# Second expert layer and output of a soft mixture of experts: halves of the columns become quarters, and all first-layer work comes ahead of it

## The chip, the cores and the metric

One core of one Trainium2 chip runs one program. The metric is the device time of one execution in microseconds (us). The kernel before took 386.4 us (median of three runs, 386.28 to 388.14). A difference of 0.5% is 1.9 us.

## The reference

Block-causal attention (blocks of 64), and a soft mixture of experts on its output; the change touches only the experts and what follows them. All values are float32.

```python
# attention: B=8, H=8, S=576, D=64 -> x of (N=4608, 512), N = B*S
logits = x @ phi                                   # (4608, 32): 8 experts x 4 slots
d = softmax(logits, axis=0);  slot_input = (d.T @ x).reshape(8, 4, 512)
for e in range(8):
    h = np.maximum(slot_input[e] @ w1[e], 0.0)     # w1[e]: (512, 1024), 2 MB
    slot_out[e] = h @ w2[e]                        # w2[e]: (1024, 512), 2 MB
c = softmax(logits, axis=1)
out = c @ slot_out.reshape(32, 512)                # (4608, 512), 9.4 MB
```

## The kernel before

The kernel has two parts. The attention part runs a software pipeline over 32 pairs of heads; every operation has a due time in a table (`TM`), and a sort of these times gives each engine's order. It also makes the logits, the 32 slot inputs (`acc`, `acc4`), and `c_all`, the weights of the last softmax. The change leaves all of that alone. The second part begins at line 683; there each engine's order is the order of the Python text.

**Weights.** Both layers' weights are 32 pieces of 1 MB (128 x 2048 floats), loaded by `load_piece` on SP's queue, in the order of their numbers. Pieces 0 to 14 go to space kept free for them during the attention part. Pieces 15 to 21 go to the attention part's own buffers as these fall free. Pieces 22 to 31 go to the places of pieces that `up` has read: `use(i)` issues the next load as soon as piece i is consumed, and once all 32 are issued it puts the place into the list `free`. The first place of `free` becomes the second `hT`; the other five are the ring `stage`, from which results are written out.

**First layer.** `up(qd, nh, c)` handles four experts (`qd`), half of the 1024 hidden columns (`nh`) and a quarter of the contraction (`c`): four matmuls of 512 columns side by side, each in 32 columns of the array. After the fourth `c`, ACT applies the relu (`hr`, line 800). `turn(qd, nh)` transposes the result on PE (line 805), and DVE copies it into `hT` (line 810).

**Second layer.** `down(qd, f, u)` multiplies one of eight slices of the hidden columns, for four experts, into half `u` of the 512 output columns: four matmuls of 256 columns side by side. Sixteen such steps make one half, summed in a PSUM bank `so[u]`. `copy_so` copies it to SBUF on DVE, and `finish` folds the four groups with one matmul (line 753) and an ACT copy (`s4`, line 756).

**Output.** `emit(u, i)` multiplies `cT` (the transposed softmax weights of two batches) or `cT4` (the 64 last rows of all batches) by `s4[u]`: four banks of PSUM (`ps_x`), each in a row group of 32 of the array. ACT copies banks 0 and 2 to a buffer of `stage`, DVE banks 1 and 3, and one DMA on SP's queue writes 1 MB (i under 4) or 0.5 MB (i = 4). All four banks of `ps_x` are in use in one `emit`, so the next one waits for these copies.

**Order.** `up` of the first four experts; then their eight `down` steps for half 0; `combine` of the second four batches' softmax; `up` of the other four experts; the other eight `down` steps for half 0; and then `STEPS` spreads the sixteen `down` steps of half 1 between the five `emit` of half 0. The five `emit` of half 1 follow. `turn_c(1)`, which makes the second `cT`, stands in the second group of `down` steps for half 0.

An fp32 matmul shows as two records in the trace: a step of four matmuls is eight records.

## Time and profile before

| | |
|---|---|
| median of 3 runs | 386.4 us |
| the profiled execution's own time | 387.56 us |
| its span, first to last instruction | 385.8 us |
| share of TensorE's full clock granted, mean | 0.978 |
| PE, DVE, ACT, POOL busy | 365.4, 286.7, 278.1, 182.0 us |
| moved by DMA | 72.27 MB, of which 9.44 MB written |

The shares are means over the attention part and the experts. The experts' part is the last 60 us, from about 327 us on, and the rows below are nearly all from there. Times in the rows are us from the span's start.

### The profile page before, as it was taken

How to read it: one execution, taken by the hardware profiler on the slowest of the kernel's cores; microseconds unless marked ns; L12 is line 12 of the kernel's file. 1: busy time of each engine (PE TensorE's matmuls, PEld its weight loads, DVE VectorE, ACT ScalarE, POOL GpSimd, SP SyncE). 2: the span in 40 equal slices, each digit the busy share in tenths (PEclk: the TensorE clock that was granted, in tenths of full speed). 3: DMA queues.
4: the chain of work that ended last, by engine and by line, in shares of the span. 5: the costliest groups of instructions: out<-in, count | busy, mean ns of one | idle time of the engine just before them, and what ended most of it. 6: DMA issues, size and time to landing. Idle time of an engine off the chain costs nothing.

```text
span 385.8 us, 14041 instructions
## 1 busy us (share of the span) xinstructions
PE 365.4 (95%) x5487; PEld 241.8 (63%) x5487; DVE 286.7 (74%) x851; ACT 278.1 (72%) x883; POOL 182.0 (47%) x349
## 2 busy tenths in 40 slices
PE   7799999999999999999999999999999989999974
PEld 2466677667767776777667766766776655344542
DVE  3577779887988898889888988898889866041552
ACT  2687888988898889788888888888888854211441
POOL 5465665555555555555555555555555442010000
PEclk9699999999999999999999999999999999999995
DMA  5326366353564563535636635453332289799797
GB/s 158 93 63 209 108 216 197 101 203 98 199 206 105 201 197 98 211 92 197 216 92 211 198 102 194 119 187 97 93 95 65 88 305 358 297 426 406 290 373 329
DMA packets 28786, 72.27 MB, mean 187 GB/s; under 512 B 6832, under 2 KB 15152, under 8 KB 23600
## 3 DMA queue, kind: packets, MB, share of 16 engines
q1 hardware_dynamic: 28720, 71.38, 53.7%
q8 instruction: 43, 0.70, 0.7%
q14 instruction: 23, 0.19, 0.1%
HBM read 61.93 MB, written 9.44 MB: 185 GB/s over the span
## 4 chain that ended last, share of the span: by engine, by line
PE 89%; ACT 4%; DVE 3%; issue 2%; POOL 0%; ACTq 0%; POOLq 0%; DVEq 0%
PE x L424 19%; PE sc L312 16%; PE pt_e L386 11%; PE sc L333 11%; PE x L434 6%; PE pt_o L386 5%; PE so L819 4%; PE hp L792 4%; PE o L770 3%; PE x L553 3%; PE x L453 2%; PE x L571 2%; ACT arena L242 1%; PE x L283 1%; ACT arena L357 1%
## 5 line engine op out<-in xcount | busy, mean ns | idle before, releaser
L369 POOL TENSOR_SCALAR arena<-arena,stat 128x512 f32<-128x512 f32 (+6 forms) x288 | 152.6, 548 | 135.3 <-DVE stat L364 129.8
L357 ACT ACTIVATE arena<-sc,stat 128x512 f32<-128x512 f32 (+6 forms) x288 | 154.6, 550 | 20.9 <-DVE stat L347 18.5
L347 DVE TENSOR_REDUCE stat<-sc 128x1 f32<-128x512 f32 (+6 forms) x256 | 131.6, 541 | 4.3 <-PE sc L333 1.9
L386 PEld LDWEIGHTS pt_e<-ident,arena 64*128 64x128 f32 x800 | 63.7, 139 | 47.5 <-issue 30.9
L242 ACT COPY arena<-pt_e 128x384 f32<-128x384 f32 (+2 forms) x127 | 63.4, 500 | 24.2 <-PE pt_o L386 23.0
L386 PE MATMUL pt_e<-ident,arena 64*128 64x64 f32 x800 | 74.8, 228 | 5.0 <-ACT arena L242 3.5
L424 PE MATMUL x<-arena 128*64 128x256 f32 (+2 forms) x640 | 76.1, 384 | 0.4 <-DVE arena L244 0.4
L386 PE MATMUL pt_o<-ident,arena 64*128 64x64 f32 x800 | 74.7, 228 | 0.0
L312 PE MATMUL sc<-arena 64*128 64x512 f32 (+1 forms) x256 | 67.1, 598 | 0.8 <-ACT arena L357 0.7
L386 PEld LDWEIGHTS pt_o<-ident,arena 64*128 64x128 f32 x800 | 62.7, 139 | 0.2
L357 ACT ACTIVATION_READ_ACCUMULATOR arena<-sc,stat 128x1 f32 x288 | 61.2, 212 | 0.0
L424 PEld LDWEIGHTS x<-arena 128*64 128x64 f32 x640 | 41.0, 137 | 30.6 <-issue 18.2
L333 PE MATMUL sc<-arena 64*64 64x288 f32 (+4 forms) x768 | 45.7, 344 | 2.9 <-ACT arena L357 2.9
L333 PEld LDWEIGHTS sc<-arena 64*64 64x64 f32 x768 | 38.4, 134 | 12.1 <-issue 6.3
L242 ACT COPY arena<-pt_o 128x512 f32<-128x512 f32 (+1 forms) x63 | 33.8, 537 | 10.0 <-PE x L424 9.4
L244 DVE COPY arena<-pt_o 128x320 f32<-128x320 f32 (+1 forms) x65 | 33.9, 521 | 4.9 <-PE pt_o L386 3.0
L244 DVE COPY xT<-x 128x64 f32<-128x64 f32 (+1 forms) x42 | 19.0, 453 | 12.2 <-PE x L424 11.9
L363 DVE TENSOR_SCALAR stat<-stat 128x2 f32<-128x2 f32 (+1 forms) x96 | 26.4, 275 | 2.1 <-ACT arena L357 2.1
L434 PE MATMUL x<-arena 128*64 128x64 f32 x640 | 25.7, 227 | 0.0
L312 PEld LDWEIGHTS sc<-arena 64*128 64x128 f32 x256 | 20.6, 192 | 6.3 <-issue 2.4
L276 POOL TENSOR_SCALAR arena<-arena 128x576 f32<-128x576 f32 x32 | 21.6, 674 | 3.0 <-DMA arena<-in_k 3.0
L434 PEld LDWEIGHTS x<-arena 128*64 128x64 f32 x640 | 21.2, 137 | 2.2
(142 smaller groups left out, 343.8 us busy)
## 6 DMA issues: line engine op xcount, KB each, us to landing
arena<-in_w SPq DMA_DIRECT2D x32, 1024.0 KB, 6.7
arena<-in_k SPq DMA_DIRECT2D x32, 288.0 KB, 3.7
arena<-in_q SPq DMA_DIRECT2D x32, 288.0 KB, 3.0
arena<-in_v SPq DMA_DIRECT2D x32, 256.0 KB, 3.1
out<-arena SPq DMA_DIRECT2D x8, 1024.0 KB, 4.7
arena<-in_v SPq DMA_DIRECT2D x32, 32.0 KB, 2.7
out<-arena SPq DMA_DIRECT2D x2, 512.0 KB, 4.6
arena<-in_phi SPq DMA_DIRECT2D x1, 64.0 KB, 3.1
```

The source lines that it names most:

```text
L242: nc.scalar.copy(out=out, in_=in_)
L244: nc.vector.tensor_copy(out=out, in_=in_)
L276: nc.gpsimd.tensor_scalar(out=area(f"ks{m % NQB}"), in0=area("kr"), scalar1=SCALE, scalar2=0.0, op0=ALU.mult, op1=ALU.add)
L312: nc.tensor.matmul(scores(t + str(j)), lhsT=q[r, lo:lo + 128], rhs=k[r, 0:NC[t]], start=True, stop=True)
L333: nc.tensor.matmul(o, lhsT=a, rhs=b, start=True, stop=True)
L347: nc.vector.tensor_reduce(out=st[:, 0, u:u + n], in_=sc, axis=AX.XY if x == "8" else AX.X, op=ALU.max, negate=True)
L357: nc.scalar.activation(out=pr, in_=sc, func=AF.Exp, bias=st[:, 0, u:u + 1], accum_out=st[:, 1, u:u + 1],)
L363: nc.vector.tensor_scalar(out=st[:, 2, c], in0=st[:, 1, c], scalar1=EPS, scalar2=None, op0=ALU.add)
L369: nc.gpsimd.tensor_scalar(out=pr, in0=pr, scalar1=st[:, 2, u:u + 1], scalar2=0.0, op0=ALU.mult, op1=ALU.add)
L386: nc.tensor.transpose(out=ptb[i][:, 64 * n:64 * n + 64], in_=prob(m, x)[r, 128 * c:128 * c + 128], identity=ident[r, r],)
L424: nc.tensor.matmul(xps[m, 0][64 * j:64 * j + 64, lo:hi], lhsT=vs(m)[:, j, c, :], rhs=rhs, start=a, stop=z, skip_group_check=True,)
L434: nc.tensor.matmul(xps[m, 1][64 * j:64 * j + 64, 0:64], lhsT=vs(m)[:, j, c, :], rhs=arena[:, lo:lo + 64], start=(c == 0), stop=(c == NQ - 1),)
```

## The change

The first layer of all eight experts comes first: pieces 0 to 15 are now w1, 16 to 31 w2. The second layer and the output go by four quarters of 128 columns (`NU`, `CW`) instead of two halves of 256. `down(u, n)` handles quarter u with steps n = 0 to 15 over both groups of experts, four matmuls of 128 columns each; the last step also copies `so` to SBUF. One `emit` now covers four batches for its quarter (the two that make 1 MB before are four by half the width), and the 64 last rows of all batches go out for two quarters at a time, after quarters 1 and 3. There are still ten transfers out, eight of 1 MB and two of 0.5 MB, and 32 loads of 1 MB. The order of the end is written out in `ENDING`: a number is so many `down` steps, "f1" is `finish(1)`, "21" is `emit(2, 1)`, "c" is `turn_c(1)`. `finish` takes its bank from the pool of `up` (`ps_h`), and `emit(3, 1)` takes two banks of that pool and two of `so`'s.

```diff
-STEPS = (2, 2, 3, 3, 3, 3, 0)
+NU = 4
+CW = 128
+ENDING = (2, "f0", 2, "00", 4, "c", 2, "01", 6, 2, "f1", 2, "10", 6, "11", 6, 2, "f2", 2, "20", 6, "21", 6, "12", "f3", "30", "31", "32")
...
-        ps_o = c2.enter_context(tc.tile_pool(name="ps_o", bufs=1, space=PSUM))
+        ps_o = c2.enter_context(tc.tile_pool(name="ps_o", bufs=2, space=PSUM))
...
-            ps = ps_x.tile([128, 512], F32, tag="x", name=f"s4_ps{u}")
+            ps = ps_h.tile([128, 512], F32, tag="h", name=f"s4_ps{u}")
...
-            n = 512 if i < 4 else 256
-            pss = [ps_x.tile([128, 512], F32, tag="x", name=f"o_{u}_{i}_{g}") for g in range(4)]
-            for x in range(n // 256):
+            if (u, i) == (NU - 1, 1):
+
+                pss = [ps_h.tile([128, 512], F32, tag="h", name=f"o_{u}_{i}_{g}") for g in range(2)]
+                pss += [ps_o.tile([128, 512], F32, tag="so", name=f"o_{u}_{i}_{g}") for g in range(2, 4)]
+            else:
+                pss = [ps_x.tile([128, 512], F32, tag="x", name=f"o_{u}_{i}_{g}") for g in range(4)]
+            todo = [(cT[i][:, x, :], s4[u]) for x in range(4)] if i < 2 else [(cT4, s4[u - 1]), (cT4, s4[u])]
+            n = CW * len(todo)
+            for x, (a, c) in enumerate(todo):
...
-        def down(qd, f, u):
-            half = slice(256 * u, 256 * u + 256)
+        def down(u, n):
+            qd, f = divmod(n, 8)
+            if n == 0:
+                so[u] = ps_o.tile([128, 512], F32, tag="so", name=f"so{u}")
+            i = 16 + 4 * u + n // 4
             for g in range(4):
-                rhs = pieces[8 + f][:, g, half] if qd == 0 else pieces[24 + 4 * u + f // 2][:, 4 * (f % 2) + g, :]
                 nc.tensor.matmul(
-                    so[u][NS * g:NS * (g + 1), :], lhsT=hTs[qd][:, f, g, :], rhs=rhs,
-                    start=(qd == 0 and f == 0), stop=(qd == 1 and f == 7), tile_position=(0, NS * g),
-                )
+                    so[u][NS * g:NS * (g + 1), 0:CW], lhsT=hTs[qd][:, f, g, :], rhs=pieces[i][:, 4 * (n % 4) + g, :],
+                    start=(n == 0), stop=(n == 15), tile_position=(0, NS * g),
+                )
+            if n == 15:
+                so_sb[u] = t2.tile([128, CW], F32, tag="so_sb", name=f"so_sb{u}", bufs=2)
+                nc.vector.tensor_copy(out=so_sb[u], in_=so[u][:, 0:CW])
...
             for c in range(4):
                 up(qd, 0, c)
+                if qd == 1 and c == 1:
+                    turn(0, 1)
...
             if qd == 0:
-                for f in range(8):
-                    down(0, f, 0)
-                    if f == 0:
-                        turn(0, 1)
                 for i in range(2):
                     combine(t2, nc.vector, 1, i)
...
-        for f in range(8):
-            down(1, f, 0)
-            if f == 1:
+        for n in range(16):
+            down(0, n)
+            if n == 3:
                 turn(1, 1)
-            if f == 4:
+        steps = [(u, n) for u in range(1, NU) for n in range(16)]
+        for x in ENDING:
+            if x == "c":
                 turn_c(1)
-        copy_so(0)
-        ahead(STEPS[0])
-        finish(0, so_sb[0])
...
+            elif isinstance(x, str) and x[0] == "f":
+                finish(int(x[1]))
+            elif isinstance(x, str):
+                emit(int(x[0]), int(x[1]))
+            else:
+                for u, n in steps[:x]:
+                    down(u, n)
+                del steps[:x]
```

The host's reordering of w1, w2 and of the result is adapted; no size in bytes changes.

## Rows read from the trace of the kernel before

**Rows 1.** Table by stretches of the end of the span. Columns: stretch in us, its length, then busy us (and number of records) of PE, PE's weight loads, DVE, ACT and POOL, the granted TensorE clock, the busy share of the DMA engines, GB/s.

```profile
329.00:331.00 2.00, 2.00 (x21) 0.68 (x25) 0.00 (x0) 0.70 (x2) 0.00 (x0) 1.00 0.04 16
331.00:356.00 25.00, 24.62 (x287) 10.30 (x283) 5.83 (x23) 4.39 (x8) 1.22 (x2) 1.00 0.99 409
356.60:360.00 3.40, 3.40 (x60) 2.17 (x56) 1.29 (x2) 1.07 (x2) 0.00 (x0) 1.00 0.09 36
360.00:371.00 11.00, 9.39 (x139) 4.92 (x131) 5.76 (x11) 4.95 (x11) 0.00 (x0) 1.00 1.00 411
371.00:373.00 2.00, 1.76 (x16) 1.22 (x16) 1.16 (x2) 0.65 (x2) 0.00 (x0) 1.00 0.58 236
373.00:384.00 11.00, 6.40 (x40) 4.34 (x40) 4.23 (x8) 3.78 (x8) 0.00 (x0) 0.62 0.99 406
384.00:385.80 1.80, 0.00 (x0) 0.00 (x0) 0.00 (x0) 0.00 (x0) 0.00 (x0) 0.50 0.01 5
```

**Rows 2.** SP's queue in order of time: start, length, issuing line, what, number of transfers. Line 191 loads weights, lines 781 and 783 write results.

```profile
330.20 7.06 SPq L191 DMA_DIRECT2D arena<-in_w  x8
342.42 1.19 SPq L191 DMA_DIRECT2D arena<-in_w  x2
359.25 2.85 SPq L781 DMA_DIRECT2D out<-arena  x2
361.75 2.86 SPq L781 DMA_DIRECT2D out<-arena  x2
368.36 0.33 SPq L783 DMA_DIRECT2D out<-arena  x1
371.64 0.33 SPq L781 DMA_DIRECT2D out<-arena  x1
...
380.59 0.33 SPq L783 DMA_DIRECT2D out<-arena  x1
```

**Rows 3.** The chain that ended last, in order of time: start, length, engine, tile and line, number of records.

```profile
329.14 5.29 PE hp L792 x48
334.43 0.59 PE hT L805 x4
335.02 1.90 PE hp L792 x16
...
352.05 0.59 PE cT_ps L715 x4
352.63 0.20 PE cT_ps L725
...
355.13 0.63 PE s_ps L753 x2
...
356.76 1.08 PE o L770 x16
357.83 1.43 PE so L819 x24
359.27 1.10 PE o L770 x16
```

**Rows 4.** The same chain, earlier: matmuls with 128, 64 and 32 columns; the first two in column groups of 32 of the array, as `down`, the third with a full array of 128 weight columns.

```profile
320.57 0.35 PE x L453 x8
320.93 0.49 PE x L463 x32
327.43 0.81 PE siT_ps L696 x8
```

**Rows 5.** Instructions of the stretch from 329 to 386 us by line and shape: number, busy us and mean ns of one, idle time before them and what ended it.

```profile
L779 DVE COPY arena<-o 128x512 f32<-128x512 f32 x16 | 10.4, 687 | 12.1 <-PE o L770 12.0
L777 ACT COPY arena<-o 128x512 f32<-128x512 f32 x16 | 8.7, 588 | 11.1 <-PE o L770 7.3 <-issue 2.9 <-ACT arena L777 0.9
L779 DVE COPY arena<-o 128x256 f32<-128x256 f32 x4 | 1.6, 422 | 1.1 <-PE o L770 1.1
L861 DVE COPY so_sb<-so 128x256 f32<-128x256 f32 x2 | 0.8, 425 | 3.4 <-PE so L819 3.4
L756 ACT COPY s<-s_ps 128x256 f32<-128x256 f32 x2 | 0.7, 372 | 2.9 <-PE s_ps L753 2.9
L728 ACT COPY cT<-cT_ps 128x64 f32<-128x64 f32 x2 | 0.4, 218 | 0.0
```

**Rows 6.** Instructions in order of time, DVE and PE: start, length, engine, line, operation, out<-in, number, idle before.

```profile
328.34 0.29 DVE L699 COPY siT<-siT_ps 128x128 f32<-128x128 f32 x1 [1.51 <-PE siT_ps L696]
356.69 1.15 PE L770 MATMUL o<-s,cT 32*128 32x256 f32 x16
359.20 1.17 PE L770 MATMUL o<-s,cT 32*128 32x256 f32 x16
366.76 0.71 PE L770 MATMUL o<-s,cT 32*128 32x256 f32 x8
369.08 1.15 PE L770 MATMUL o<-s,cT 32*128 32x256 f32 x16 [0.46 <-ACT s L756]
```

**Rows 7.** Table as in rows 1, single microseconds.

```profile
356.00:357.00 1.00, 1.00 (x20) 0.50 (x16) 0.00 (x0) 0.17 (x1) 0.00 (x0) 1.00 0.68 279
360.00:361.00 1.00, 1.00 (x24) 0.45 (x20) 0.60 (x1) 0.64 (x2) 0.00 (x0) 1.00 0.94 393
375.00:376.00 1.00, 0.71 (x7) 0.63 (x8) 0.94 (x2) 0.72 (x2) 0.00 (x0) 0.84 1.10 459
```

## The prediction

> **What bounds it now.** I read the table by stretches first [rows 1]. From 331 to 356 us the DMA engines are busy 0.99 of the time, from 356.6 to 360 only 0.09, then 1.00, 0.58 for two microseconds, 0.99 to 384, and nothing in the last 1.8. So the end is a transfer of weights, a hole, and a transfer of results. PE is busy through the hole: it works off what must come before the first result. SP's queue [rows 2] says what opens and closes the hole. Line 191 loads at 330.20 and after; these are the ten pieces that wait for `up` to free places. The first result is issued at 359.25, and data moves from about 360.1 (0.94 busy in that microsecond [rows 7]), 0.85 us after the issue. The ten loads run from about 331.2 (0.99 of the 25 us from 331 on [rows 1]) to 356.7 (0.68 busy in that microsecond [rows 7]): 25.5 us, 2.55 us a megabyte.

> With these sizes the end of the kernel before can be rebuilt. Results start at 360.1, nine megabytes take 22.95 us, the second hole costs 0.42 of 2 us, 0.84: 383.9. Data ends at 384.0, the span 1.8 later. So three things set the end: when the first result is issued, whether results are then made every 2.55 us, and the two fixed lags. Two bounds follow: the loads end at 356.7 whatever is done after 330, since `up` of the first four experts frees the places at the same times in both kernels; and the results need 22.95 us behind them. No order can end before 356.7 + 22.95 + 1.8 = 381.45, 4.35 under the span.

> The chain [rows 3] shows what PE does before the first result: `up` from 329.14, transposes, `down` for half 0 in two groups, `turn_c`, the fold (0.63), the first `emit` at 356.69 [rows 6].

> **The change, part by part: the work up to the first result.** Sizes first. Six `up` steps take 5.29 us [rows 3], 0.87 each without the start, four times 0.215 us for two passes of 256 columns; so 0.107 us for 128 columns of one pass. Three old `down` steps (24 records) take 1.43 us [rows 3]: six times 0.215, and 0.14 for going from one shape of array to another. A new `down` step has half the columns. Does it take half the time? The nearest rows are line 453, 128 columns in the same column groups (0.35 us for eight records alone, start and end included), and line 463, 64 columns: 32 records in 0.49 us, 0.12 a step of eight, as long as its columns take (0.107) within a tenth [rows 4]. I take 0.215 for a new step, so 64 new steps cost what 32 old ones did; k steps in one block cost 0.215 k + 0.14.

> In the new order PE goes on at 336.7, behind the first eight `up` (335.02 + 1.90, less 0.2 in which the last matmul drains [rows 3]). Then: eight more `up`, 7.0; three `turn` of 0.59 [rows 3], 1.8, and 0.1 for the last relu; sixteen `down` steps of quarter 0, 3.45; three changes of shape that the sums don't hold yet, 0.4. That is 349.4 at most, and 349.3 is taken. Removed from this path: half the columns of the sixteen old `down` steps, and `turn_c` (0.59 + 0.20 [rows 3]). Nothing here waits for a piece: 0 to 21 have landed by 329 (DMA 0.04 busy from there [rows 1]). `combine` now stands ahead of `turn(0, 1)`'s copies on DVE, four operations of about 0.8 us; what waits behind them is the second half of `hT` for the first experts, wanted only in the fifth `down` step, five microseconds later. So I cost it at nothing. If that cover were gone it would cost the two microseconds by which `combine` outlasts the transposes.

> Then two `down` steps (0.57), `finish` (one matmul in two passes of 128 columns, 0.215, and 0.2 around it: the old 0.63 less 0.215 [rows 3]), two `down` steps. The copies of 128x128 take 0.29 on DVE [rows 6], on ACT between 0.22 (64 wide) and 0.37 (256 wide) [rows 5]; the two blocks cover each. First `emit` at 350.9, against 356.69: 5.8 us sooner. From an `emit`'s first matmul to its DMA issue it is 2.56 us now (356.69 to 359.25, 359.20 to 361.75, 369.08 to 371.64 [rows 2, 6]), two pairs of copies of 0.69 on DVE [rows 5] among it. First result issued at 353.5, before the loads have ended. The first hole is gone.

> **The work between results.** An old `emit` holds PE 1.10 us [rows 3]: four groups of 0.215 and 0.24. A new one has eight groups of 0.107, each with weights of its own, 128 columns. Line 696 loads such weights for eight records in 0.81 us, 0.10 a record [rows 4], so that load and stream take about the same; if they overlap, as they must in the old `emit` (four groups of 0.215 + 0.10 would make 1.26 before any start, and it took 1.08 to 1.10 in all), 1.10 stays. That is taken; if they don't, it is 1.10 + 8 x 0.10 = 1.9.

> [...]

> Now `ENDING`, as start times of the emits on PE. "01" comes behind 1.10, four steps 1.0, "c" 0.79, two steps 0.57: 354.35. "10" comes behind 1.10, eight steps 1.86, fold 0.42, two steps 0.57: 358.3. "11": 1.10 + 1.43, 360.85; the four banks are free then, since old emits stand 2.51 apart with the same copies [rows 6]. "20": 364.8. "21": 367.35. "12", half an `emit`, 0.66: 369.9. "f3" 0.42; its copy on ACT waits behind those of "12" (two of 0.37), and what waits behind it is "30": 371.7. Issues: 353.5, 356.9, 360.9, 363.4, 367.4, 369.9, 371.5 (half: 366.76 to 368.36, 1.60 [rows 2, 6]), 374.3, and then, as "31" has banks of its own and DVE works without a pause, 375.6 and 376.4 (+ 1.37 and + 0.84). The other banks thus save the wait for copies; I cost that at nothing, since "30" is still being sent for 2.55 us.

> Data, at 0.85 behind an issue and 2.55 a megabyte, in order: "00" 356.7 to 359.25, "01" to 361.8, "10" to 364.35, "11" to 366.9. "20" can start only at 368.25: a hole of 1.35. It ends 370.8, "21" 373.35, "12" 374.6; "30" starts at 375.15, a hole of 0.55, and with "31" and "32" ends at 381.5. The span ends at 383.3. Holes after the first result come to 1.9 us against 0.84 before: a pair of emits takes PE 6.5 us, its transfer 5.1. Of the 4.35 that the bound allows, 2.5 are won.

> **Rivals.** First, results without a hole: if a pair of emits is made faster by a microsecond than summed (the 0.14 and 0.2 around blocks overlap more), the span ends at 381.45 to 382.4, 4.35 to 3.4 under before: 382.0 to 383.0. For it speaks that most starts were counted as in isolation; against it, that they were taken from rows.

> Second, the hand-offs give it back. Twenty blocks stand between 350.9 and "30", most of them a change of shape, and each extra 0.1 us moves the end by 2.0. At 0.07 to 0.15 more (a start of 0.21 to 0.29 instead of 0.14, or copies of 0.29 that two short steps don't cover), the median is 385.3 to 386.9. The fold of 0.63 with its 0.2 around it [rows 3] shows that such sizes occur.

> [...]

> Third, slower: the weights of an `emit` are not hidden at 128 columns. "30" then starts six and a half emits later by 0.8 us each, 5.2: the span ends at 388.5, the median at 389.1. It decides from 0.69 us an emit on (0.5% slower), and gives the whole gain back at 0.39. Against it speaks the overlap in the old `emit`.

> The clock: it fell from 1.00 to 0.84 in the microsecond from 375 and then to half, after PE had work for 9.39 of 11 and 1.76 of 2 us [rows 1, 7]. The new order keeps PE in work until 374.9 or so, and I count no loss. At half clock from 371 on, "30" would be issued 1.1 later, and so would the end be.

> **How the numbers follow.** The sum is against the profiled execution: 385.8 span, 387.56 us of its own time, 1.8 around it. The median of the three runs is 386.4, so I take the difference: 386.4 - 2.5 = 383.9. Own range of this case 383.0 to 385.3. Chances: this 0.48; no hole 0.17; hand-offs 0.25; weights not hidden 0.10. From 381.8 (under the bound by 0.2) to 386.6 about 8 in 10 are held: all of the first two, most of the third, none of the last. Faster by over 0.5% (under 384.5, about what a measurement of this kernel can tell from no change): 0.17 and four fifths of 0.48, 0.56. Slower: the last, 0.09. The rest, 0.35, is within 0.5%.

> **What would show it.** In the profile after: `up` ends near 345 and the first result is issued at 353 to 354; DMA is busy without a pause from 331 to about 366.5; emits of a pair start 2.5 us apart and the first of two pairs 6.5; a short hole stands ahead of the fifth transfer. Wrong would be: an `emit` that holds PE 1.5 us or more (third rival), a new `down` step over 0.25, DMA idle between 357 and 366 (second rival), or loads that end later than 357, on which the bound rests.

## The result and the profile after

Before, the median is 386.48 us (385.94 to 388.64, 17 runs); after, 389.28 us (388.59 to 390.67, 17 runs). The ratio is 1.0064, with a 95% interval of 1.0049 to 1.0079: slower by 0.6%, where I had forecast 0.6% faster. The profiled execution of after took 389.62 us, with a span of 387.8.

Its attention part, which the change leaves alone, happened to end 0.63 us sooner: the first `up` matmul starts at 328.45 us instead of 329.07. Where I set a forecast time beside a measured one below, the forecast is moved by that. Counted from that matmul, the rest took 56.7 us before and 59.4 after; 54.2 was forecast.

TensorE's instructions from the first `emit` on, in order of time: start, length, line, tile, number of matmul records, and in brackets the idle time ahead of the group and what ended it. Line 778 is `emit`, 831 `down`, 754 the fold.

```profile
350.25 1.16 PE L778 MATMUL o<-s,cT 32*128 32x128 f32 x28
352.51 0.49 PE L778 MATMUL o<-s,cT 32*128 32x128 f32 x4 [1.10 <-issue]
...
355.30 1.23 PE L778 MATMUL o<-s,cT 32*128 32x128 f32 x32
356.46 1.29 PE L831 MATMUL so<-arena 128*32 128x128 f32 x39
358.84 0.52 PE L831 MATMUL so<-arena 128*32 128x128 f32 x9 [1.08 <-issue]
...
363.28 0.49 PE L778 MATMUL o<-s,cT 32*128 32x128 f32 x5
364.21 1.16 PE L778 MATMUL o<-s,cT 32*128 32x128 f32 x27 [0.44 <-issue]
...
368.23 0.93 PE L778 MATMUL o<-s,cT 32*128 32x128 f32 x19
369.59 0.72 PE L778 MATMUL o<-s,cT 32*128 32x128 f32 x13 [0.43 <-issue]
...
371.68 1.17 PE L778 MATMUL o<-s,cT 32*128 32x128 f32 x32
372.79 1.52 PE L831 MATMUL so<-arena 128*32 128x128 f32 x48
374.23 0.73 PE L778 MATMUL o<-s,cT 32*128 32x128 f32 x16
...
375.89 3.28 PE L778 MATMUL o<-s,cT 32*128 32x128 f32 x80 [0.51 <-ACT s L758]
```

The first `emit` stands at 350.25; 350.9 less 0.63 is 350.27. So everything up to there was summed right. An undisturbed `emit` is 32 matmul records and 1.1 to 1.2 us long, and the next block starts 1.11 behind it (371.68 to 372.79). But four blocks are cut in two, in the middle: the first `emit` after 28 of its 32, the `down` steps behind "01" after 39, "11" after 5, "20" after 19. Ahead of the second piece stands "issue", which means that the engine waited for nothing that the profile shows: no semaphore, no other engine, no bank (the one stop of another kind, ahead of the last line, waits for ACT's copy of the fold). The weight loads stop with the matmuls, which the same view of their queue shows:

```profile
352.51 0.30 PEld L778 LDWEIGHTS o<-s,cT 32*128 32x128 f32 x3 [1.29 <-issue]
358.84 0.25 PEld L831 LDWEIGHTS so<-arena 128*32 128x32 f32 x9 [1.35 <-issue]
364.21 0.42 PEld L778 LDWEIGHTS o<-s,cT 32*128 32x128 f32 x12 [0.63 <-issue]
369.59 0.53 PEld L778 LDWEIGHTS o<-s,cT 32*128 32x128 f32 x13 [0.62 <-issue]
```

What the stops do to the transfers is seen in the table by stretches, as in [rows 1, 7] (stretch, length, busy us of PE, its weight loads, DVE, ACT and POOL, granted clock, DMA share, GB/s):

```profile
353.00:361.00 8.00, 6.92 (x175) 5.36 (x179) 2.27 (x4) 2.55 (x6) 0.00 (x0) 1.00 0.99 401
361.00:364.00 3.00, 2.77 (x85) 2.26 (x81) 1.29 (x2) 1.07 (x2) 0.00 (x0) 1.00 0.20 79
366.00:368.00 2.00, 2.00 (x62) 1.64 (x55) 0.82 (x2) 0.52 (x2) 0.00 (x0) 1.00 0.68 266
370.00:372.00 2.00, 2.00 (x65) 1.68 (x63) 1.29 (x2) 1.07 (x2) 0.00 (x0) 1.00 0.06 16
```

The old hole at 357 [rows 1] is gone, as forecast. In its place stand three, of about 2.4, 0.6 and 1.9 us (length times one less the share), ahead of the third, fourth and fifth result; of these three places the forecast had a hole only at the last, of 1.35 us.

Where the stops come from is told by two lines of the page, the instructions of each engine and the DMA queues by kind. Before:

```profile
PE 365.4 (95%) x5487; PEld 241.8 (63%) x5487; DVE 286.7 (74%) x851; ACT 278.1 (72%) x883; POOL 182.0 (47%) x349
q8 instruction: 43, 0.70, 0.7%
```

After:

```profile
PE 362.5 (93%) x5891; PEld 247.8 (64%) x5891; DVE 286.7 (74%) x853; ACT 278.1 (72%) x885; POOL 182.0 (47%) x349
q8 instruction: 46, 0.75, 0.8%
```

Queue 8 carries instructions: 43 packets for 10,974 records of PE and its weight loads before, 46 for 11,782 after, one for 255 or 256 records on the mean, 16 KB each. Counted in the records of after, the four stops are 255, 256 and 256 apart, one packet's worth each. The packet with the next block starts 2.9 to 4.0 us after PE has begun the block before it (3.31, 4.02, 3.10, 2.89), and PE goes on 2.3 to 2.5 us after the packet's start (2.39, 2.31, 2.28, 2.48): 5.4 to 6.3 us a block. The new kernel uses one up sooner: an `emit` and six `down` steps are 64 + 96 = 160 records, weight loads among them, in 2.55 us (371.68 to 374.23), so 256 in 4.1. Before, an `emit` and three `down` steps held 32 + 48 = 80 in 2.51 us [rows 6], so 256 in 8.0.

A block's packet comes while the block before it runs, and this throughout the profile: of the 46 packets of after, 45 start when TensorE has begun the block before theirs, one 0.96 us ahead of that, and none a block earlier.

### The profile page after: what moved, and what is told of

Its sections match the earlier page's. It is cut to its first block, busy times and chain, and to the rows that moved or that the text cites. A ratio compares the mean times of both kernels' runs of the same rounds, so it can differ in the third digit from the quotient of the medians.

```text
span 387.8 us, 14854 instructions
## 1 busy us (share of the span) xinstructions
PE 362.5 (93%) x5891; PEld 247.8 (64%) x5891; DVE 286.7 (74%) x853; ACT 278.1 (72%) x885; POOL 182.0 (47%) x349
## 5 line engine op out<-in xcount | busy, mean ns | idle before, releaser
L428 PEld LDWEIGHTS x<-arena 128*64 128x64 f32 x640 | 41.0, 137 | 30.6 <-issue 18.2
L337 PE MATMUL sc<-arena 64*64 64x288 f32 (+4 forms) x768 | 44.9, 340 | 3.2 <-ACT arena L361 3.2
L787 DVE COPY arena<-o 128x512 f32<-128x512 f32 (+1 forms) x20 | 11.7, 632 | 16.4 <-PE o L778 16.4
(142 smaller groups left out, 360.9 us busy)
```

What stands on the lines that cost most here:

```text
L337: nc.tensor.matmul(o, lhsT=a, rhs=b, start=True, stop=True)
L428: nc.tensor.matmul(xps[m, 0][64 * j:64 * j + 64, lo:hi], lhsT=vs(m)[:, j, c, :], rhs=rhs, start=a, stop=z, skip_group_check=True,)
```

## The experiments

**The same program, shifted.** Thirty-two small matmuls, 64 records with their weight loads, at the start.

```diff
+        def pad():
+            nc.tensor.matmul(xps["w"][:, 0:64], lhsT=idle[:, 0:128], rhs=idle[:, 128:192], start=True, stop=True)
...
+        for i in range(32):
+            at(-49 + 0.01 * i, pad)
```

> 32 small matmuls on zeros are put at the very start, where PE waits for the first loads; they are 64 more PE instructions ahead of everything else. Theory A (PE runs out of instructions: they come in blocks of 256, and in the dense part it gets through a block before the next has come): the four stops of the changed kernel move up the program by 64 instructions. They stood inside emit 00 (28 of 32 records done), in the eight down steps behind emit 01 (39 of 64 done), in emit 11 (5 done) and in emit 20 (19 done); now they stand in the two down steps ahead of emit 00, in the same eight down steps but with about 7 of 64 done, in the six down steps behind emit 10 (about 20 of 48), and in the two down steps ahead of emit 20. Together 3 to 4.5 us as before, the time within 1 us of the changed kernel's 389.3. Theory B (a wait of the program itself: a bank, a copy, a buffer that is not free): the stops stay at the same matmuls of the program, the same lengths.

It took 390.08 us (389.30 to 391.06, 5 runs), ratio to before 1.0086. TensorE, as above (836 is `down`, 783 `emit` here):

```profile
350.44 0.63 PE L836 MATMUL so<-arena,hT 128*32 128x128 f32 x12
352.32 0.41 PE L836 MATMUL so<-arena,hT 128*32 128x128 f32 x4 [1.25 <-issue]
352.67 1.17 PE L783 MATMUL o<-s,cT 32*128 32x128 f32 x32
...
357.31 0.42 PE L836 MATMUL so<-arena 128*32 128x128 f32 x7
358.51 1.39 PE L836 MATMUL so<-arena 128*32 128x128 f32 x41 [0.78 <-issue]
```

The first two stops stand at the same numbers of instruction as in after, counted from the program's start, and so at other instructions: the first `emit` is whole, and the two `down` steps ahead of it are cut. Neither `emit` nor `down` stops by itself; the place in the program does it. The size did not come out as expected: the third and fourth stop are missing (their packets started 1.29 and 1.36 us after the block before had begun, instead of 3.10 and 2.89), one of under 0.5 us stands among the last emits instead, and yet the kernel is no faster than after. In its profile "30" starts 45.4 us behind the first `up` matmul, 2.0 sooner than in after, but from there to the span's end it is 13.1 us instead of 11.95. Most data has ended by 384.5, but some of the DMA engines run on to 386.2 (0.45 busy in the microsecond from 384, 0.09 in the next). Why the last transfer straggles there I can't say.

**Fewer instructions for the same `emit`.** The operands are exchanged: the 128 columns of `s4` become the weights, the four batches of `cT` the 512 moving columns. A 1 MB `emit` is 16 records instead of 64, with the same columns streamed; the host's reordering follows.

```diff
-            todo = [(cT[i][:, x, :], s4[u]) for x in range(4)] if i < 2 else [(cT4, s4[u - 1]), (cT4, s4[u])]
-            n = CW * len(todo)
+            todo = [(s4[u], cT[i].rearrange("p b s -> p (b s)"))] if i < 2 else [(s4[u - 1], cT4), (s4[u], cT4)]
+            m = 512 if i < 2 else 128
+            n = m * len(todo)
...
```

> emit with its operands exchanged: the folded result is loaded as weights once for each row group, and the softmax weights of four batches stream as 512 columns, so the 1 MB emits have 16 PE instructions instead of 64 with the same columns streamed; the result comes out transposed and the host puts it in order. Theory A: one pair of an emit and six down steps is 112 instructions in 2.5 us instead of 160; the stops shrink from 3.9 us to under 1, emit 30 starts at about 371 to 372 instead of 375.9, the time is 384.3 to 386.3. Theory B: the banks, copies and buffers are the same, the stops stay, 389. Third: the new order is slow for another cause (transfers, copies): 388 to 389.5.

It took 386.36 us (385.22 to 388.89, 10 runs): ratio to before 1.0001 [0.9978, 1.0024], 2.9 us less than after. TensorE:

```profile
350.56 0.85 PE L832 MATMUL so<-arena,hT 128*32 128x128 f32 x20
352.03 0.63 PE L832 MATMUL so<-arena,hT 128*32 128x128 f32 x12 [0.62 <-issue]
...
358.02 1.71 PE L779 MATMUL o<-cT,s 32*128 32x512 f32 x8
359.66 1.08 PE L832 MATMUL so<-arena,hT 128*32 128x128 f32 x32
...
361.10 1.14 PE L779 MATMUL o<-cT,s 32*128 32x512 f32 x8
362.18 1.52 PE L832 MATMUL so<-arena 128*32 128x128 f32 x48
```

An undisturbed `emit` is as long as before (1.14 us; the next block 1.08 behind it). With six `down` steps it is now 112 records, weight loads among them, 256 in 5.8 us. The third and fourth stop are gone. The second has shrunk and shows no idle time: in the `emit` at 358.02 the fourth row group starts 0.57 us behind the other three, 255 records behind the first stop and 2.5 us behind the start of a packet, and the next block stands 1.64 us behind instead of 1.08. The two stops left come to 1.2 us, a little more than the 1 us expected at most. The first one stays: ahead of it stand the sixteen `down` steps of quarter 0, 256 records in some 3.5 us besides the transposes between them.

**The dense blocks spread.** The `down` steps of the first four experts for quarters 0 and 1 stand between the `up` steps of the others, where a block of 256 records lasts longest (an `up` step's 16, weight loads among them, take 0.87 us [rows 3], so 256 take 13.9). No instruction is added or left out.

```diff
...
+        def early(k):
+            if k < 4:
+                down(0, k)
+            else:
+                down(0, k)
+                down(1, 2 * (k - 4))
+                down(1, 2 * (k - 4) + 1)
...
+                if qd == 1:
+                    early(c)
...
```

> The changed kernel with its instructions spread more evenly: the down steps of the first four experts for quarters 0 and 1 stand between the up steps of the other four (each up step is 16 instructions in 0.87 us, each down step 16 in 0.215). Same work, same order of results. Theory A: from emit 00 on 128 instructions fewer; the stops fall from 3.9 to 1.5 to 3 us, the time is 386.5 to 388.5; emit 00 starts about 1.5 us later, which the transfers hide. Theory B: stops as before, 389 to 390.5.

It took 386.19 us (384.65 to 387.87, 10 runs), ratio to before 0.9976 [0.9955, 0.9996]: 3.1 us less than after with the same instructions. TensorE:

```profile
351.18 1.17 PE L778 MATMUL o<-s,cT 32*128 32x128 f32 x32
...
359.65 0.49 PE L778 MATMUL o<-s,cT 32*128 32x128 f32 x5
360.31 1.16 PE L778 MATMUL o<-s,cT 32*128 32x128 f32 x27 [0.17 <-issue]
...
364.32 0.93 PE L778 MATMUL o<-s,cT 32*128 32x128 f32 x19
365.96 0.72 PE L778 MATMUL o<-s,cT 32*128 32x128 f32 x13 [0.71 <-issue]
```

The first two stops went, and the two of the later, still dense stretch stayed, after 5 records of "11" and 19 of "20" as in after. The time is 0.3 us under the range expected.

**The banks of "31" undone.** "31" takes its banks from `ps_x` like the others.

```diff
-            if (u, i) == (NU - 1, 1):
+            if False:
```

> The last part undone: emit 31 takes the same four banks as all others. By the prediction's costing: emit 31 waits for the copies of 30 (about 0.75 us), its transfer is issued later by as much, and the transfer of 30 (2.55 us) covers it: the time stays within 0.5 us of the changed kernel. Rival: the last transfers are not queued behind each other, then 0.7 to 1.5 us slower. The four stops of PE are unchanged in either case.

It took 389.17 us (388.12 to 390.21, 6 runs), as after (389.28). The emits "20", "31" and "32" on TensorE:

```profile
369.00 1.26 PE L778 MATMUL o<-s,cT 32*128 32x128 f32 x32
...
377.72 2.48 PE L778 MATMUL o<-s,cT 32*128 32x128 f32 x32 [0.70 <-ACT arena L785]
380.51 1.71 PE L778 MATMUL o<-s,cT 32*128 32x128 f32 x15 [0.31 <-ACT arena L785]
```

In after the last three run as one block of 3.28 us; here "31" and "32" wait for copies, and part of their time runs at a granted clock of 0.50 (from 379 on; the mean of the profiled run is 0.979, of after's 0.990). By the medians it costs nothing that can be measured. But one expectation failed: only three of the four stops are there, "20" is whole. So "30" starts 0.6 us sooner behind `up` than in after, and the part behind "30" takes 12.6 us instead of 11.95: a cost of 0.6 for the banks could be hidden here. It also shows that which stops come can differ from one profile to the next without a change in the program ahead of them. That one stop is missing in one profile proves little by itself; the times of many runs have to bear it out.

**The second layer thinned.** A `down` step is 8 records instead of 16, each matmul one bf16 pass of 512 columns over zeros: the same time on TensorE (six steps 1.41 us, 368.83 to 370.24, against 1.44 in after), but the second layer's result is left out.

```diff
-                    so[u][NS * g:NS * (g + 1), 0:CW], lhsT=hTs[qd][:, f, g, :], rhs=pieces[i][:, 4 * (n % 4) + g, :],
+                    so[u][NS * g:NS * (g + 1), :], lhsT=idle[:, 0:NS],
+                    rhs=idle[:, 128:192].unsqueeze(1).broadcast_to([128, 8, 64]),
```

> The changed kernel with the down steps thinned: each of the four matmuls of a step is one bf16 matmul of 512 columns on zeros (a tile of zeros as weights and as data) in place of the fp32 matmul of 128 columns, so PE streams for the same time (0.215 us a step) with 8 instructions instead of 16; the second layer is left out by this and the written result is zero. The rest, the transfers among it, is unchanged. Theory A (instructions come too late): a pair of an emit and six down steps is 112 instructions in 2.5 us; the stops fall from 3.9 us to under 1, the time is 384.5 to 386.5. Theory B (waits of the program): stops as before, 389.

It took 384.64 us (383.86 to 386.81, 10 runs) against 386.86 of the kernel before on that chip (385.46 to 389.63, 35 runs): ratio 0.9954 [0.9928, 0.9980]. TensorE, and the table by stretches at the end:

```profile
351.22 1.17 PE L778 MATMUL o<-s,cT 32*128 32x128 f32 x32
352.33 1.05 PE L831 MATMUL so<-idle 128*32 128x512 bf16 x16
...
371.90 3.28 PE L778 MATMUL o<-s,cT 32*128 32x128 f32 x80 [0.51 <-ACT s L758]
```

```profile
361.00:364.00 3.00, 3.00 (x72) 1.79 (x64) 1.62 (x4) 1.07 (x2) 0.00 (x0) 1.00 1.01 421
381.00:382.00 1.00, 0.00 (x0) 0.00 (x0) 0.00 (x0) 0.00 (x0) 0.00 (x0) 0.50 0.66 266
382.00:383.00 1.00, 0.00 (x0) 0.00 (x0) 0.00 (x0) 0.00 (x0) 0.00 (x0) 0.50 0.07 29
```

With `emit` as in after, no block is cut, and the transfers run through 361 to 364, where after has 0.20. This is the chain that I had summed, without the stops. Start to start on TensorE, in us:

| | forecast | after | thinned |
|---|---|---|---|
| "00" to "01" | 3.45 | 5.05 | 3.42 |
| "01" to "10" | 3.95 | 5.43 | 4.04 |
| "10" to "11" | 2.55 | 2.55 | 2.51 |
| "11" to "20" | 3.95 | 4.95 | 3.99 |
| "20" to "21" | 2.55 | 3.45 | 2.51 |
| "21" to "12" | 2.55 | 2.55 | 2.55 |
| "12" to "30" | 1.80 | 1.66 | 1.66 |
| sum | 20.80 | 25.64 | 20.68 |
| "30" to the span's end | 11.6 | 11.95 | 12.65 |

The intervals of after that hold a stop are longer by 1.63, 1.39, 0.96 and 0.94 us than the thinned ones, 4.92 in all. The thinned ones are within 0.09 of the forecast, but for the last, which is 0.14 shorter.

**Without the first six results.** Their transfers are left out, so after the loads the queue is empty until "12".

```diff
-            if i < 2:
+            if u < 3 and i < 2:
+                pass
+            elif i < 2:
```

> The changed kernel without six of its ten transfers out (those of emits 00 to 21; these rows of the result are left unwritten), so that behind the last load, at about 356, the DMA queue is empty until emit 12. Theory A1 (the block of instructions is late because its own transfer waits behind data in the DMA engines): its fetches behind 357 start 1.0 to 1.6 us after the block before them has begun, and the stops in emits 11 and 20 are gone; those in emit 00 and behind emit 01 stay, 1.2 us each. Theory A2 (the fetch is that slow by itself): all four stops stay, fetches start 3 to 4 us after the beginning of the block. The time itself says nothing, since the transfers are left out.

It took 386.20 us (385.32 to 388.74, 8 runs), a time that can't be set beside the others, as less is written. TensorE (833 is `down`):

```profile
348.98 1.16 PE L778 MATMUL o<-s,cT 32*128 32x128 f32 x28
351.22 0.49 PE L778 MATMUL o<-s,cT 32*128 32x128 f32 x4 [1.08 <-issue]
...
355.18 1.29 PE L833 MATMUL so<-arena 128*32 128x128 f32 x39
357.01 0.51 PE L833 MATMUL so<-arena 128*32 128x128 f32 x9 [0.54 <-issue]
...
361.45 1.18 PE L778 MATMUL o<-s,cT 32*128 32x128 f32 x32
...
365.48 1.17 PE L778 MATMUL o<-s,cT 32*128 32x128 f32 x32
```

The two stops beside the weight loads stay; the two beside the missing results are gone ("11" and "20" are whole). In the records, the instruction packets start 3.26 and 3.47 us after their block's predecessor began while the loads run, and 1.13, 1.11, 0.37 and 0.13 us after it when next to nothing else moves. The attention parts of the ten profiles agree. Of their 380 packets, 45 had a DMA share of data under 0.05 from the block's start to their own: they came at most 1.9 us after it (median 1.0). The 82 with a share over 0.9 came after 0.3 to 6.2 us (median 3.5). So the fetch comes later while data moves, and with dense instructions that wait reaches TensorE. It does not come late each time: in the shifted kernel the third packet started 1.29 us into its block beside a share of 0.9, and in the kernel with all of it together, below, two started after 0.69 and 0.30 us beside 0.9 to 1.0.

In the trace a transfer of 1 MB is 128 records of 8 KB, on the mean eight for each of the 16 engines, of 0.31 us each. Eight of them come to 2.5 us, an estimate from these figures, and full queues add 2 to 3 us here. Whether the one is the cause of the other no run here tests.

**All of it together.** The exchanged `emit`, the spread `down` steps, and `finish(3)` ahead of "12" with the other banks given to "30".

```diff
...
-ENDING = (2, "f0", 2, "00", 4, "c", 2, "01", 6, 2, "f1", 2, "10", 6, "11", 6, 2, "f2", 2, "20", 6, "21", 6, "12", "f3", "30", "31", "32")
+ENDING = (2, "f0", 2, "00", 2, "c", 2, "01", 2, "f1", 2, "10", 6, "11", 6, 2, "f2", 2, "20", 6, "21", 6, "f3", "12", "30", "31", "32")
...
-            if (u, i) == (NU - 1, 1):
+            if (u, i) == (NU - 1, 0):
...
```

> Both remedies together (operands of emit exchanged, down steps spread among the up steps), and at the end f3 ahead of emit 12, with the other banks given to emit 30, so that the copy of f3 is covered by emit 12. Theory A: stops under 0.7 us in all; from the first up to the last instruction 54 to 55.5 us (before 56.7, changed 59.4); the time is 383.8 to 385.3 beside 386.4 of before. Otherwise 386 or more.

It took 384.51 us (383.88 to 386.86, 12 runs): ratio to before 0.9939 [0.9913, 0.9965], 2.35 us faster than before, where the exchanged `emit` alone had 1.0001 and the spread steps alone 0.9976. What the place of `finish(3)` and the banks add to that was not run by itself. The table by stretches:

```profile
353.00:361.00 8.00, 7.92 (x147) 4.43 (x143) 4.16 (x7) 4.19 (x9) 0.00 (x0) 1.00 1.00 412
361.00:364.00 3.00, 3.00 (x73) 2.00 (x74) 1.58 (x3) 1.07 (x2) 0.00 (x0) 1.00 0.97 399
366.00:368.00 2.00, 2.00 (x57) 1.50 (x56) 1.29 (x2) 1.08 (x2) 0.00 (x0) 1.00 0.55 221
```

TensorE has work for 7.92 of 8 us where after had 6.92, and only one hole of about 0.9 us is left, ahead of the fifth result, where the forecast had put one of 1.35. No stop for instructions is left.

**The order alone.** The kernel before with the new order of the first layer, halves and `STEPS` kept.

```diff
-                rhs = pieces[8 + f][:, g, half] if qd == 0 else pieces[24 + 4 * u + f // 2][:, 4 * (f % 2) + g, :]
+                rhs = pieces[16 + 8 * u + 4 * qd + f // 2][:, 4 * (f % 2) + g, :]
...
-                for f in range(8):
-                    down(0, f, 0)
...
+        for f in range(8):
+            down(1, f, 0)
...
```

> The order alone: all first-layer work ahead of the second layer, w1 in pieces 0 to 15, but halves of 256 columns, the emits and their order as in the kernel before. Theory A: the down steps of 256 columns need 16 instructions in 0.43 us, no stops; PE has the same work ahead of emit 00 as before, so the time is that of before, 385.9 to 387. Rival (the new order itself costs, through combine ahead of the transposes or the places of the weights): 388 to 389.5.

It took 386.20 us (385.30 to 388.23, 10 runs), ratio to before 0.9988 [0.9963, 1.0013]: no change. Its first `emit`:

```profile
356.43 1.15 PE L770 MATMUL o<-s,cT 32*128 32x256 f32 x16
```

The first `emit` stands where it stood (356.69 [rows 6]), since the same `down` work comes before it. What brings it forward is the narrower first part, the quarter.

## Why the prediction was wrong

**The work up to the first result: right.** The start of "00" on TensorE came out to 0.02 us; sixteen new `down` steps cost what eight old ones did, `combine` stood on DVE at no cost, and the hole of [rows 1] closed.

**"A new `emit` holds PE 1.10, a `down` step 0.215": right for each, wrong as a sum.** Undisturbed they measured 1.11 and about 0.22 (six steps with the change of shape 1.44 us, 372.79 to 374.23, against 1.43). The step that failed is the one that went from durations to start times: it took it for granted that TensorE always has its next instruction. Halving the columns halves the time of a step (0.43 us before [rows 3], 0.22 now), keeps its records (16, weight loads among them), and so doubles the records per microsecond; the sum saw only the first. The count of records was in the rows, but I priced an instruction at its duration alone. From the first `emit` to "30" after takes 4.84 us more than forecast; the gain forecast was 2.5. The four stops are 3.9 us of it as idle time (of the weight loads), and each of the three cut emits lasts 0.3 us longer beside that: the first has the next block 2.68 us behind it instead of 1.11, of which 1.29 is idle. In the profiled execution the miss of the part from `up` on is 59.4 - 54.2 = 5.2, of which 0.35 lies behind "30".

**The end of the data: a little short.** From "30" to the span's end I had 11.6 us; 11.95 after, and 12.65 in the thinned kernel, though its last results were issued as early as the forecast has them. There the bulk had ended at 382, which is where the sum puts it, and the rest trickled to about 383. The fixed lag of [rows 1] doesn't hold such a straggler.

**The rivals.** None was the right one. The slower one gave 389.1, close to the 389.28 measured, and for a wrong reason: an undisturbed `emit` holds PE 1.11 us at 128 columns, with 1.0 us of weight loads in that time (32, from 371.7 to 372.7), and 1.10 at 256 [rows 3]. So its weights are hidden at both widths; 1.9 was summed for the case that they are not. The sign that I had named for the hand-offs, DMA idle between 357 and 366, did come, but the hand-offs were sized right (the table above): the sign did not belong to that cause alone.

**The costs put at nothing.** The other banks: right by the medians (389.17 without them), though up to 0.6 us could be hidden there. The clock: right, 1.00 on the path, and down to 0.77 and then 0.50 only in the microseconds from 383 and 384, after the last `emit`.

**The idea itself was worth its forecast.** Without stops, thinned or rearranged, the quarters gained 2.2 and 2.35 us; 2.5 was forecast. The first of these leaves the second layer's result out, the second has a further change at the end, so each is a near figure and not the forecast case itself. I had a range whose upper end, 386.6, lay 2.7 us too low because the case that happened had no place among the cases.

## What to carry to other kernels

When a change cuts instructions smaller, count the records per microsecond of the dense stretch beside their durations, and compare them with what the page shows of instruction fetches: here 256 records (a 16 KB packet) took 5.4 to 6.3 us where the fetch came late beside transfers, and TensorE was through with them in 4.1. A group cut in two with "issue" ahead of its second half, at equal distances in the engine's count of instructions (255, 256 and 256 in after), is the mark of it; where the cut fell between row groups that run side by side, only the time to the next block showed it (1.64 us instead of 1.08 with the operands exchanged). The cure here was fewer instructions for the same columns (the longer operand as the moving one, 2.9 us less than after), or sparse work mixed into the dense (3.1 less).
